# Two attention blocks in one kernel: another order of the second block's two-step cycle, with the last two heads' row maxima taken together in every other step

## The chip, the cores and the metric

The kernel runs on 1 core of one Trainium2 chip. The metric is device time in microseconds (us). The time before is 1884.33 us, the median of 3 runs (1877.62 to 1885.6).

Engines are named as in the profile: PE (TensorE matmul), PEld (its weight loads), DVE (VectorE), ACT (ScalarE), POOL (GpSimd), SP (the engine that issues the DMAs).

## The reference

Two independent multi-head attentions, each with its own input of 2048 tokens by 512 and its own weights, 32 heads of 16. Block A looks back over a window of 256 keys, block B over all 2048 keys. Their outputs are joined along the last axis.

```python
def _B_ref(x, wqkv, wo):
    B, S, D = x.shape            # 1, 2048, 512
    H = 32
    Dh = D // H
    qkv = (lambda x, *d: x.transpose(*d))((x @ wqkv).reshape(B, S, 3, H, Dh), 2, 0, 3, 1, 4)
    q, k, v = qkv[0], qkv[1], qkv[2]
    scores = jnp.einsum("bhqd,bhkd->bhqk", q, k) * (Dh ** -0.5)
    p = _softmax(scores, axis=-1)
    o = jnp.einsum("bhqk,bhkd->bhqd", p, v)
    return (lambda x, *d: x.transpose(*d))(o, 0, 2, 1, 3).reshape(B, S, D) @ wo
```

`_A_ref` is the same with scores outside the window set to -1e9.

## The kernel before

Work is cut into units: a block, a group of 4 heads, and a chunk of 512 queries. Each block has 8 groups x 4 chunks = 32 units. Block A's units and most projections come first, in an order written out by hand; block B's attention follows in the loop at the end of `attention_kernel` (lines 1009 to 1060), which the change touches.

In block B a unit is 16 steps, one for each tile of 128 keys. What belongs to a step:

- **s** (`scores`, line 501): for one head, a matmul of keys by queries into one PSUM bank (128 keys x 512 queries), then an exponential on ACT (line 508) into the tile `p`. Three banks ("e", 0 to 2) serve in turn. Four s make a step.
- **a digit** (`weigh2`, line 532): the weighted sums of values with the exponentials of two steps earlier; 4 stands for all four quarters of the queries, 2 for two of them. Its result gathers in bank 3 ("o") and is copied out by ACT at the unit's end (line 558).
- **M and m** (`max2`, lines 372 and 376): the row maxima of the *next* unit, which the softmax needs ahead of its scores. An item is 128 queries by 512 keys for the four heads of the group: PE makes the products (line 372), DVE reduces them (line 376). M takes heads 0 and 1 together into banks 4 and 5 and reduces them with one instruction. m takes one head, in turn 2 and 3, into one of the banks 6 and 7 (`room()`, which alternates between them). There is an item in every step, 16 in a unit.

When the 16 items of a unit are done, `max_finish` (line 435) takes the maximum over the key chunks (line 444, DVE) and splits it into three parts on POOL. Two steps later `max_rows` (line 463) runs ahead of the step's first s: a transpose on PE (line 468) into one of the banks 6 and 7, again by `room()`, a copy on ACT (line 470) and two DMAs that write the result as extra rows beside the queries.

The heads of a group lie on two sets of rows: even heads at rows 0 to 50, odd heads at rows 64 to 114 (`ROW = 0, 64`). Heads 0 and 2 thus share the first rows, 1 and 3 the second.

The string `ORDER` sets the order in which PE gets this work; it holds two steps (eight s, eight quarters, two items) and is repeated until all items are done. Then `LAST` takes over, without maxima. Each engine works off its own queue in order, and the waits between engines follow from the tiles and banks that are read and written.

```python
ORDER = "ssm4mssMs2msms2sM"
...
            elif x in "Mm" and nm < len(mx):
                u, g, c, qt, kc = mx[nm]
                if x == "M":
                    h = (0, 1)
                    two = view(("p", 0))
                else:
                    h = (2 + half,)
                    half ^= 1
                    two = room()[1][:, None]
                max2(g, c, qt, kc, h, two)
```

`view(("p", 0))` is banks 4 and 5, `view(("p", 1))` banks 6 and 7.

Of the kernel before, what the change touches and what calls it, by code (L numbers as in the profile page):

```python
# [37 lines left out]
PACE = 16 * STEP  # L38


ORDER = "ssm4mssMs2msms2sM"
LAST = "ssss4"
AHEADM = 4
QU = 2.4
# [77 lines left out]
def attention_kernel(ctx: ExitStack, tc: tile.TileContext, xT, wqk, wv, wo, out):  # L122
# [74 lines left out]
    def view(bank):  # L197
        pool, n = bank
        first, width = {"e": (0, 1), "o": (3, 1), "p": (4, 2), "s": (6, 1)}[pool]
        n = first + width * n + (pool == "e" and n > 2)  # L200
        return ps_all[:, n] if width == 1 else ps_all[:, n:n + 2]
# [159 lines left out]
    def max2(g, c, qt, kc, heads, ps):  # L361

        m = maxima(1, g, c).rearrange("p (a r) q k -> p a r q k", a=2)
        early = g == 0 and c == 0 and heads[0] < 2
        if not early:
            follow(("k", 1, g))
            follow(("q", 1, g, c))
        for n, j in enumerate(heads):
            r, a = divmod(j, 2)
            rows = slice(ROW[a], ROW[a] + KS)  # L370
            q, k = (qe[0], ke()) if early else (opq[1, g, c][:, r], opk2(g)[:, r])
            nc.tensor.matmul(ps[:, n], q[rows, 128 * qt:128 * qt + 128], k[rows, kc * QC:kc * QC + QC], start=True,  # L372
                             stop=True)
            t = M.pe("h", 118, 0 if early else loaded(1, g, c))
        r, a = divmod(heads[0], 2)
        nc.vector.tensor_reduce(out=m[:, a:a + len(heads), r, qt, kc], in_=ps, axis=AX.X, op=ALU.max)  # L376
        return M.run("DVE", 65 + 533 * len(heads), t)
# [85 lines left out]
    def max_rows(b, g, c):  # L463
        n = f"{b}_{g}_{c}"
        nm = parts["nm"]
        bank, ps = room()
        ps = ps.bitcast(BF16)
        nc.tensor.transpose(ps[:48, :128], nm.rearrange("p a s j q -> p (a s j q)"), ident)  # L468
        nt = sb.tile([48, 128], F32, name=f"ntr_{n}", tag="ntr")
        nc.scalar.activation(nt, ps[:48, :128], AF.Copy)  # L470
        t = M.run("ACT", 200, M.pe("f", 60, ready["nm", b, g, c]))
        release(bank, t)
        for a in range(2):
            ready["q", b, g, c] = M.dma(12, t)
            nc.sync.dma_start(opq[b, g, c][ROW[a] + KS:ROW[a] + KM].bitcast(F32).rearrange(
                "s r (q t) -> s (r q) t", t=128), nt[24 * a:24 * a + 24])
# [14 lines left out]
    def scores(b, g, c, kt, j, heads=1, pieces=((),)):  # L491

        n = f"{b}_{g}_{c}_{kt}"
        pr, a0 = divmod(j, 2)
        banks = [M.take("e") for _ in range(heads)]
        ps = [view(bank) for bank in banks]
        w = QC if b else sum(x[3] for x in pieces)
        for k, col, q0, n1 in [(kt, 0, 0, QC)] if b else pieces:
            for x in range(heads):
                rows = slice(ROW[a0 + x], ROW[a0 + x] + KM)  # L500
                nc.tensor.matmul(ps[x][:, col:col + n1], opk2(g)[rows, pr, 128 * k:128 * k + 128],  # L501
                                 opq[b, g, c][rows, pr, q0:q0 + n1], start=True, stop=True)
            t = M.pe("h", 235 if b else 12 + n1 / 2.4, ready["q", b, g, c])
        if a0 == 0:
            pts[b, g, c, kt, pr] = sb.tile([128, 2, QC], F32, name=f"p_{n}_{pr}", tag="p", bufs=2 * AHEAD)
        p = pts[b, g, c, kt, pr]
        for x in range(heads):
            nc.scalar.activation(p[:, a0 + x, :w], ps[x][:, :w], AF.Exp, scale=SCALE)  # L508
            done = M.run("ACT", 60 + w / 1.2, t)
            M.release(banks[x], done)  # L510
        if b == 0:

            for d, sign, base in ((0, 1, 0), (2, -1, -1)):
                cols = [col // 128 + x for k, col, q0, n1 in pieces for x in range(n1 // 128)
                        if 4 * c + q0 // 128 + x - k == d]
                for x in cols:
                    v = p[:, :, 128 * x:128 * x + 128]
                    nc.gpsimd.affine_select(out=v, in_=v, pattern=[[0, 2], [sign, 128]], compare_op=ALU.is_ge,  # L518
                                            fill=zero_fill, base=base, channel_multiplier=-sign)
                    done = M.run("Pool", 360, done)  # L520
        ready["p", b, g, c, kt] = done

    def weigh2(g, c, kt, q0, q1):

        follow(("v", 1, g // 2))
        if kt == 0 and q0 == 0:
            obank[0] = M.take("o")
            pvt[1, g, c] = view(obank[0])
        o = pvt[1, g, c]
        for j in range(HG):  # L530
            vc = VW * (HG * (g % 2) + j)
            nc.tensor.matmul(o[32 * j:32 * j + 32, q0:q1], vt[(g // 2) % 2][:, kt, vc:vc + 32],  # L532
                             pts[1, g, c, kt, j // 2][:, j % 2, q0:q1], start=kt == 0 and q0 == 0,
                             stop=kt == NT - 1, skip_group_check=True)
        M.pe("c", 1.7 * (q1 - q0) + 50, ready["p", 1, g, c, kt], ready["v", 1, g // 2, kt])
# [147 lines left out]
    def settle():  # L683

        while soon and soon[0][0] <= M.t["PE"]:
            heapq.heappop(soon)[2]()
# [18 lines left out]
    def room():  # L705

        if slot[0]:
            slot[1] ^= 1
            return None, view(("s", slot[1]))
        while bank() >= M.NEVER:  # L710
            advance()
        b = M.take(pool())
        return b, view(b)[:, 0] if b[0] == "p" else view(b)
# [5 lines left out]
    def pop():  # L719
        now[0], _, f, a = heapq.heappop(todo)  # L720
        f(*a)
        made.add((f, *a))
# [149 lines left out]
    nm = k = nb = ne = 0  # L872
# [18 lines left out]
    while todo_a or gen[0]:  # L891
# [7 lines left out]
        x = "p" if gen[0] else todo_a[0]  # L899
# [105 lines left out]
    mx = [(NA + 1 + i // 16, *units[NA + 1 + i // 16][1:], *divmod(i % 16, NQC)) for i in range(16 * turn)]  # L1005
    ns, nq, nm, half, got = 0, -8, AHEADM, 0, 0
    t0 = M.t["PE"]
    rows = []
    while nq < 4 * len(steps):
        if nm == len(mx) and len(M.banks["e"]) == 3:  # L1010
            M.banks["e"] += [M.t["PE"]] * 2
        for x in ORDER if nm < len(mx) else LAST:
            k = ns // HG
            if x == "s" and k < len(steps):
                if ns % HG == 0:
                    t = k * STEP
                    M.t["PE"] = max(M.t["PE"], t0 + int(1000 * k * STEP))
                    settle()
                    while todo and todo[0][0] <= t:
                        pop()  # L1020
                    if rows and rows[0][0] <= k:
                        max_rows(*rows.pop(0)[1])
                scores(1, *steps[k], ns % HG)
                ns += 1
            elif x in "Mm" and nm < len(mx):
                u, g, c, qt, kc = mx[nm]
                if x == "M":
                    h = (0, 1)
                    two = view(("p", 0))
                else:  # L1030
                    h = (2 + half,)
                    half ^= 1
                    two = room()[1][:, None]
                max2(g, c, qt, kc, h, two)
                got += len(h)
                if got == HG:
                    nm += 1
                    got = 0
                    if nm % 16 == 0:
                        max_finish(1, g, c)  # L1040
                        rows.append((k + 2, (1, g, c)))
            elif x.isdigit():
                if 0 <= nq < 4 * len(steps):
                    g, c, kt = steps[nq // 4]
                    q = nq % 4
                    weigh2(g, c, kt, 128 * q, 128 * (q + int(x)))
                    if kt == NT - 1 and q + int(x) == 4:
                        unit_end(1, g, c)
                nq += int(x)
                if int(x) == 4:  # L1050

                    t = k * STEP
                    two = heapq.nsmallest(2, proj)
                    if two and two[-1][0] <= t and max(operands(y[3]) for y in two) <= M.t["PE"]:
                        now[0] = t
                        for _ in two:
                            advance()
                            while gen[0]:
                                advance()
                            t0 += 2400  # L1060
# [29 lines left out]
```

## Time and profile before

| | |
|---|---|
| median of 3 runs | 1884.33 us (1877.62 to 1885.6) |
| the profiled execution | 1874.48 us |
| its span, first to last instruction | 1872.8 us |
| granted TensorE clock, mean | 0.995 |
| PE / DVE / ACT / POOL busy, share of the span | 98% / 83% / 75% / 25% |
| last maxima of block B's loop | at about 1782 us of the span |

The profile is of one execution. A row of the groups reads: line, engine, operation, tile written <- tiles read, shapes, count | busy time in all, mean ns of one | idle time of the engine ahead of them and what ended it. The chain of waits is the work that ended last, followed back: each piece with its start, its length and what it was. In a timeline the rows are in order of start, and equal instructions that overlap or follow each other stand in one row with their count, the start of the first and the time to the end of the last.

### The profile page before, as it was taken

What the parts mean: (1) busy time and instruction counts of PE and PEld (TensorE: products, weight loads), DVE (VectorE), ACT (ScalarE), POOL (GpSimd) and SP (SyncE); (2) the same over time, 40 slices, a digit from 0 to 9 for tenths busy, and PEclk for the clock granted to TensorE, in tenths of its full rate; (3) what the DMA queues carried; (4) which work ended last, traced back from release to release, by engine and by line L of the source; (5) the groups of instructions that cost most, each with busy time, mean ns of one, the idle gap of its engine ahead of it and who ended that gap; (6) DMA issues with size and microseconds to landing.
All of it is one profiled execution on the core that took longest, in us unless ns stands there. A gap on an engine that the chain in (4) does not pass through costs nothing.

```text
span 1872.8 us, 37299 instructions
## 1 busy us (share of the span) xinstructions
PE 1838.9 (98%) x14376; PEld 926.7 (49%) x14376; DVE 1547.6 (83%) x2320; ACT 1408.5 (75%) x2754; POOL 468.7 (25%) x896
## 2 busy tenths in 40 slices
PE   8999989999999999999999999999999999999999
PEld 6666555666664554544444444444444444444446
DVE  4666677766779777799999999999999999999911
ACT  4356655655548777788888888888888888888883
POOL 0267777655572332000000000100000000000010
PEclk9999999999999999999999999999999999999999
DMA  8665656545554222411310132121031121010102
GB/s 258 182 193 174 204 174 203 171 124 158 171 176 109 92 89 68 95 28 34 61 36 16 36 59 48 28 62 29 16 73 28 34 62 36 16 39 21 31 30 96
DMA packets 129137, 166.68 MB, mean 89 GB/s; under 512 B 22996, under 2 KB 58836, under 8 KB 128948
## 3 DMA queue, kind: packets, MB, share of 16 engines
q1 hardware_dynamic: 128960, 164.31, 30.7%
q8 instruction: 113, 1.85, 0.4%
q14 instruction: 64, 0.52, 0.1%
HBM read 94.49 MB, written 68.19 MB: 87 GB/s over the span
## 4 chain that ended last, share of the span: by engine, by line
PE 91%; DVE 5%; DMA 1%; ACT 1%; issue 1%; SPq 1%; POOL 0%; ACTq 0%; POOLq 0%
PE ps_all L532 29%; PE ps_all L372 19%; PE ps_all L186 18%; PE ps_all L501 18%; PE ps_all L547 4%; PE ps_all L420 3%; DVE mt L376 2%; DVE mt L430 1%; DVE ps_all L429 1%; ACT p L508 1%; PE ps_all L468 1%; DMA vt<-vd 1%; DVE nm L460 0%; DMA in<-xT_A 0%; DVE nr L458 0%
## 5 line engine op out<-in xcount | busy, mean ns | idle before, releaser
L508 ACT ACTIVATE p<-ps_all 128x512 f32<-128x512 f32 x2432 | 1261.5, 600 | 179.7 <-PE ps_all L501 121.0
L376 DVE TENSOR_REDUCE mt<-ps_all 128x2 f32<-128x1024 f32 x1516 | 1202.0, 866 | 79.0 <-PE ps_all L501 52.1
L501 PE MATMUL ps_all<-oq,opk 51*128 51x512 f32 (+2 forms) x2752 | 780.1, 410 | 8.6 <-ACT p L508 5.8
L372 PE MATMUL ps_all<-opk,oq 48*128 48x512 f32 x2016 | 678.1, 439 | 2.0 <-DVE mt L376 1.9
L532 PE MATMUL ps_all<-p,vt 128*32 128x256 f32 (+1 forms) x6056 | 598.3, 467 | 0.5 <-ACT ou L558 0.5
L501 PEld LDWEIGHTS ps_all<-oq,opk 51*128 51x128 f32 x2752 | 396.8, 185 | 205.4 <-ACT p L508 181.9
L372 PEld LDWEIGHTS ps_all<-opk,oq 48*128 48x128 f32 x2016 | 313.2, 185 | 319.9 <-issue 144.2
L453 POOL TENSOR_SCALAR mm<-mm 128x16 f32<-128x16 f32 x31 | 7.8, 253 | 977.5 <-PE ps_all L501 769.3
L518 POOL TENSOR_SCALAR_AFFINE_SELECT p<-p 128x256 f32<-128x256 f32 x480 | 179.6, 407 | 210.5 <-ACT p L508 148.5
L532 PEld LDWEIGHTS ps_all<-p,vt 128*32 128x32 f32 x6056 | 119.6, 108 | 219.1 <-issue 208.5
L186 PE MATMUL ps_all<-x,w 128*128 128x512 f32 x768 | 197.6, 407 | 9.0 <-ACT w L140 9.0
L429 DVE COPY_PREDICATED ps_all<-mone,ps_all 128x256 f32<-128x256 uint16 x224 | 94.8, 423 | 103.1 <-PE ps_all L420 102.5
L186 PEld LDWEIGHTS ps_all<-x,w 128*128 128x128 f32 x768 | 142.9, 192 | 49.4 <-ACT w L140 9.0
L430 DVE TENSOR_REDUCE mt<-ps_all 128x2 f32<-128x512 f32 x224 | 155.2, 693 | 7.7
L248 ACT ACTIVATE raw<-ps_all 128x512 f32<-128x512 f32 x56 | 33.5, 598 | 111.0 <-PE ps_all L186 109.3
L420 PE MATMUL ps_all<-opk,oq 48*128 48x384 f32 (+2 forms) x512 | 91.8, 377 | 9.1 <-DVE mt L430 7.8
L547 PE MATMUL ps_all<-p,vt 128*32 128x384 f32 (+2 forms) x1408 | 98.6, 393 | 0.3 <-POOL p L518 0.3
L186 PE MATMUL ps_all<-w_v,x 128*128 128x512 f32 x384 | 95.1, 398 | 0.2 <-ACT p L508 0.2
L186 PE MATMUL ps_all<-w_o,x_o 128*128 128x512 f32 x384 | 90.4, 393 | 0.0
L186 PEld LDWEIGHTS ps_all<-w_o,x_o 128*128 128x128 f32 x384 | 71.2, 188 | 23.7 <-issue 8.4
L186 PEld LDWEIGHTS ps_all<-w_v,x 128*128 128x128 f32 x384 | 70.2, 188 | 18.7 <-issue 1.9
L259 POOL TENSOR_TENSOR st<-raw,st 128x512 fp32r<-128x512 f32 x56 | 72.0, 1285 | 4.7
(58 smaller groups left out, 588.6 us busy)
## 6 DMA issues: line engine op xcount, KB each, us to landing
parts<-st SPq DMA_DIRECT2D x64, 512.0 KB
oq<-parts SPq DMA_DIRECT2D x128, 128.0 KB
opk<-parts SPq DMA_DIRECT2D x128, 128.0 KB
od<-ou SPq DMA_DIRECT2D x64, 256.0 KB
vd<-vst SPq DMA_DIRECT2D x32, 272.0 KB
oq<-parts SPq DMA_DIRECT2D x128, 64.0 KB
opk<-parts SPq DMA_DIRECT2D x128, 64.0 KB
t<-od SPq DMA_DIRECT2D x32, 256.0 KB
```

The source lines that it names most:

```text
L186: nc.tensor.matmul(ps, l(u), r(v), start=start and k == 0, stop=stop and k == n - 1)
L259: nc.gpsimd.tensor_sub(two[:, 1], raw, two[:, 0].bitcast(F32))
L372: nc.tensor.matmul(ps[:, n], q[rows, 128 * qt:128 * qt + 128], k[rows, kc * QC:kc * QC + QC], start=True, stop=True)
L376: nc.vector.tensor_reduce(out=m[:, a:a + len(heads), r, qt, kc], in_=ps, axis=AX.X, op=ALU.max)
L420: nc.tensor.matmul(two[:, a, 0:w], opq[b, g, c][rows, r, 128 * qt:128 * qt + 128], opk2(g)[rows, r, t0:t1], start=True, stop=True)
L429: nc.vector.copy_predicated(two[:, :, 256:384], later, two[:, :, 0:128])
L430: nc.vector.tensor_reduce(out=m[:, :, r, qt, 0], in_=two[:, :, 128:384], axis=AX.X, op=ALU.max)
L501: nc.tensor.matmul(ps[x][:, col:col + n1], opk2(g)[rows, pr, 128 * k:128 * k + 128], opq[b, g, c][rows, pr, q0:q0 + n1], start=True, stop= ...
L508: nc.scalar.activation(p[:, a0 + x, :w], ps[x][:, :w], AF.Exp, scale=SCALE)
L518: nc.gpsimd.affine_select(out=v, in_=v, pattern=[[0, 2], [sign, 128]], compare_op=ALU.is_ge, fill=zero_fill, base=base, channel_multiplier ...
L532: nc.tensor.matmul(o[32 * j:32 * j + 32, q0:q1], vt[(g // 2) % 2][:, kt, vc:vc + 32], pts[1, g, c, kt, j // 2][:, j % 2, q0:q1], start=kt ...
L547: nc.tensor.matmul(o[32 * j:32 * j + 32, q0:q0 + w], vt[(g // 2) % 2][:, kt, vc:vc + 32], pts[b, g, c, m, j // 2][:, j % 2, col:col + w], ...
```

## The change

The order string is another, and a new letter N takes heads 2 and 3 of an item together, into banks 6 and 7, as M does heads 0 and 1 in banks 4 and 5. In the first step of a cycle the item is M m m as before; in the second it is M N. The counts of scores, weighings and items in a cycle are the same; DVE gets five reductions in place of six.

```diff
-ORDER = "ssm4mssMs2msms2sM"
+ORDER = "sMss4msssmM2ssN2"
@@
-            elif x in "Mm" and nm < len(mx):
+            elif x in "MNm" and nm < len(mx):
                 u, g, c, qt, kc = mx[nm]
                 if x == "M":
                     h = (0, 1)
                     two = view(("p", 0))
+                elif x == "N":
+                    h = (2, 3)
+                    two = view(("p", 1))
                 else:
                     h = (2 + half,)
                     half ^= 1
```

On PE, the middle of a cycle in block B's unit of group 4, chunk 1 before the change. In `p_4_1_12_0` the numbers are group, chunk, key tile and pair of heads; line 532 weighs, line 501 makes scores, line 372 the products for the maxima:

```order
L532 MATMUL ps_all<-p_4_1_12_0_14041,vt_75 32x512 x2
L532 MATMUL ps_all<-p_4_1_12_1_14055,vt_75 32x512 x2
L372 MATMUL ps_all<-opk_73,oq_4_3_13635 128x512
L501 MATMUL ps_all<-oq_4_1_12813,opk_73 128x512 x2
L372 MATMUL ps_all<-opk_73,oq_4_3_13635 128x512 x2
L501 MATMUL ps_all<-oq_4_1_12813,opk_73 128x512
L532 MATMUL ps_all<-p_4_1_13_0_14063,vt_75 32x256 x2
L532 MATMUL ps_all<-p_4_1_13_1_14076,vt_75 32x256 x2
```

The same place of PE's order after the change:

```order
L532 MATMUL ps_all<-p_4_1_12_0_13899,vt_75 32x512 x2
L532 MATMUL ps_all<-p_4_1_12_1_13908,vt_75 32x512 x2
L372 MATMUL ps_all<-opk_73,oq_4_3_13505 128x512
L501 MATMUL ps_all<-oq_4_1_12695,opk_73 128x512 x3
L372 MATMUL ps_all<-opk_73,oq_4_3_13505 128x512 x3
L532 MATMUL ps_all<-p_4_1_13_0_13919,vt_75 32x256 x2
L532 MATMUL ps_all<-p_4_1_13_1_13933,vt_75 32x256 x2
```

Between the two weighings stood six matmuls (m s s M M s, with M as two); now there are seven (m s s s m M M).

The second place is the transpose on PE (line 468) at a cycle's start, before the change:

```order
L532 MATMUL ps_all<-p_4_1_11_1_14015,vt_75 32x256 x2
L501 MATMUL ps_all<-oq_4_1_12813,opk_73 128x512
L372 MATMUL ps_all<-opk_73,oq_4_3_13635 128x512 x2
L468 LDWEIGHTS nm_4_2_14028
L468 MATMUL ps_all<-ident,nm_4_2_14028 48x128
L501 MATMUL ps_all<-oq_4_1_12813,opk_73 128x512 x2
L372 MATMUL ps_all<-opk_73,oq_4_3_13635 128x512
L532 MATMUL ps_all<-p_4_1_12_0_14041,vt_75 32x512 x2
```

And the same transpose after it, where the `x2` of line 372 ahead of the weighing is N:

```order
L501 MATMUL ps_all<-oq_4_1_12695,opk_73 128x512 x2
L372 MATMUL ps_all<-opk_73,oq_4_3_13505 128x512 x2
L532 MATMUL ps_all<-p_4_1_11_0_13859,vt_75 32x256 x2
L532 MATMUL ps_all<-p_4_1_11_1_13873,vt_75 32x256 x2
L468 LDWEIGHTS nm_4_2_13882
L468 MATMUL ps_all<-ident,nm_4_2_13882 48x128
L501 MATMUL ps_all<-oq_4_1_12695,opk_73 128x512
L372 MATMUL ps_all<-opk_73,oq_4_3_13505 128x512 x2
L501 MATMUL ps_all<-oq_4_1_12695,opk_73 128x512 x2
L532 MATMUL ps_all<-p_4_1_12_0_13899,vt_75 32x512 x2
```

The transpose moved from the middle of a group of scores and maxima to the head of one, right behind a weighing; the last maxima ahead of it were a single and an M, and are now an N.

## The prediction

> **What bounds the kernel now.** I read the page's busy shares first, then a table of windows to find the stage that the change touches, then that stage by instruction, then the chain of waits through it, slot by slot.
>
> ```profile
> PE 1838.9 (98%) x14376; PEld 926.7 (49%) x14376; DVE 1547.6 (83%) x2320; ACT 1408.5 (75%) x2754; POOL 468.7 (25%) x896
> L376 DVE TENSOR_REDUCE mt<-ps_all 128x2 f32<-128x1024 f32 x1516 | 1202.0, 866 | 79.0 <-PE ps_all L501 52.1
> ```
>
> The page names PE, but its busy ends are modelled, so 98% is not proof. The second row counts the changed operation: 1516 row-maximum reductions. 40 of them are made ahead of the loop (32 for the first unit of block B, 8 for the next unit's first four items), which leaves 1476; at six in a cycle that is **246 cycles of the order string**. The windows (columns: length, then busy time of PE, PEld, DVE, ACT, POOL, then clock, DMA share, GB/s) and the groups of the second one, 16 units or 128 cycles long, by shape:
>
> ```profile
> 604.00:1072.50 468.50, 468.48 (x3767) 210.48 (x3766) 420.68 (x551) 384.94 (x752) 65.68 (x106) 1.00 0.20 54
> 1072.50:1682.07 609.57, 609.55 (x5139) 252.81 (x5137) 603.39 (x793) 540.86 (x1057) 42.36 (x104) 1.00 0.17 42
> ...
> L508 ACT ACTIVATE p<-ps_all 128x512 f32<-128x512 f32 x1025 | 533.3, 600 | 68.7 <-PE ps_all L501 39.4 <-PE ps_all L372 13.2
> ...
> L376 DVE TENSOR_REDUCE mt<-ps_all 128x1 f32<-128x512 f32 x512 | 327.6, 677 | 4.5 <-PE ps_all L501 3.4 <-PE ps_all L372 1.1
> L376 DVE TENSOR_REDUCE mt<-ps_all 128x2 f32<-128x1024 f32 x257 | 311.9, 1214 | 0.0
> ...
> L558 ACT ACTIVATE ou<-ps_all 128x512 f32<-128x512 f32 x16 | 9.7, 609 | 0.0
> ...
> L470 ACT ACTIVATE ntr<-ps_all 48x128 f32<-48x128 bf16 x16 | 4.1, 257 | 0.0
> ...
> L444 DVE TENSOR_REDUCE mm<-mt 128x16 f32<-128x64 f32 x16 | 3.5, 219 | 1.7
> ...
> L584 DVE RECIPROCAL rd<-ld 128x32 f32<-128x32 f32 x8 | 2.7, 339 | 0.0
> ```
>
> A cycle lasts 609.57/128 = 4.76 us, a unit of eight cycles 38.10. DVE is busy 603.39 of 609.57 us, so DVE is full as well. How long it really holds for one reduction comes from its timeline, where two that overlap stand in one row:
>
> ```profile
> 1004.47 1.27 DVE L376 TENSOR_REDUCE mt<-ps_all 128x1 f32<-128x512 f32 x2
> ...
> 1005.67 1.81 DVE L376 TENSOR_REDUCE mt<-ps_all 128x2 f32<-128x1024 f32 x2
> ```
>
> Two singles end 1.27 us after the first started; less the 0.68 of the second, they start **0.60** apart. A pair with a single behind it takes 1.81, less 0.68 is **1.13**. DVE's floor for a cycle of two pairs and four singles is 2x1.13 + 4x0.60 = 4.66.
>
> PE's floor comes from the chain of waits over one cycle (start, length, what):
>
> ```profile
> 1005.78 0.99 PE ps_all L532 x8
> 1006.78 0.42 PE ps_all L372
> 1007.20 0.24 PE ps_all L501 x2
> 1007.44 0.24 PE ps_all L372 x2
> 1007.68 0.57 PE ps_all L532 x8
> 1008.25 0.67 PE ps_all L372 x2
> 1008.92 0.57 PE ps_all L532 x8
> 1009.49 0.67 PE ps_all L501 x2
> 1010.16 0.23 PE ps_all L372 x2
> 1010.39 1.00 PE ps_all L532 x8
> ```
>
> This is 4.61 us from 1005.78 to 1010.39, with no wait in it. Sixteen score and maximum matmuls (lines 501 and 372) stand there in three groups between the weighings (line 532), and the groups take 0.90, 0.67 and 0.90. They hold 6, 4 and 6 matmuls: the first two of a group take 0.42-0.43 together, every further two 0.23-0.24. Two matmuls in the time of one are possible because even heads lie on rows 0 and up, odd heads on rows 64 and up. I call the time of such a pair a **slot**: now 3 + 2 + 3 = 8. So PE (4.61) and DVE (4.66) are within 0.05 us of each other, and an edit that helps one and hurts the other has to be counted on both.
>
> **The change, part by part.**
>
> *DVE.* In every second step two singles become a pair: 2x0.60 - 1.13 = 0.07 us saved, a cycle falls from 4.66 to 3x1.13 + 2x0.60 = 4.59. If DVE alone set the pace, that would be 246x0.07 = 17 us. [...]
>
> *PE's slots.* Matmuls issue in order. Write 0 and 1 for even and odd heads. Before, a cycle is 1 0 1 0 1 0 | 0 1 1 0 | 1 0 1 0 1 0: whoever pairs off neighbours finds 3, 2 and 3 mixed pairs. After, with the groups from the rows of the two orders:
> - s M s s: 0, 0 1, 1 0. The second 0 must wait for the first, so the first runs alone: 3 slots for five matmuls, 0.90 us.
> - m s s s m M: 0 1, 0 1, 1 0, 1. Four slots for seven, the last one alone: 0.42 + 3x0.24 = 1.13.
> - s s N: 0 1, 0 1: two slots, 0.67.
>
> That is 9 slots. The weighings stay 0.99 + 0.57 + 0.57. **PE's cycle: 4.61 + 0.235 = 4.845**, now clearly above DVE's 4.59. That a lone matmul costs a whole slot shows where a transpose cuts a group:
>
> ```profile
> 1023.49 0.42 PE ps_all L501
> 1023.91 0.23 PE ps_all L372 x2
> 1024.14 0.22 PE ps_all L468
> 1024.36 0.43 PE ps_all L501 x2
> 1024.79 0.45 PE ps_all L372
> 1025.24 1.00 PE ps_all L532 x8
> ```
>
> Here the order is s3 M0 M1, transpose, s0 s1 m. M1 has no partner and takes 0.23 on the chain. The group takes 1.75 instead of 0.90: this cut costs 0.85 in each unit today.
>
> *The transpose (line 468).* It takes a bank of the two in which the single maxima stand (banks 6 and 7). Today it waits a little for a single; the same place on both engines' timelines:
>
> ```profile
> 1023.55 0.59 PE L372 MATMUL ps_all<-opk,oq 48*128 48x512 f32 x2
> 1024.14 0.22 PE L468 MATMUL ps_all<-ident,nm 128*48 128x128 bf16 x1
> 1024.29 0.50 PE L501 MATMUL ps_all<-oq,opk 51*128 51x512 f32 x2
> ...
> 1022.28 1.81 DVE L376 TENSOR_REDUCE mt<-ps_all 128x2 f32<-128x1024 f32 x2
> ```
>
> The single behind that pair ends at 1022.28 + 1.81 = 1024.09, the transpose starts at 1024.14, and the next scores 0.15 later. After the change the two banks belong to N, the last reduction of the cycle, and only a weighing of 0.57 lies between N and the transpose. When does N end? Count from the start of the group s M s s. DVE has slack in the new cycle and waits for the first m, whose matmul starts after 0.90 + 0.99 = 1.89 and is readable about 0.53 later (0.50 a first matmul, 0.03-0.05 a semaphore, as between 1024.09 and 1024.14): 2.42. Then come m 0.60, m 0.60, M 1.13, so N starts at 4.75, ends 1.21 later at 5.96, and frees the transpose at 6.01. Its own turn would be at 4.845: it waits 1.17. Behind it in PE's queue stand all of the next cycle's matmuls, so the wait is on the path. With the 0.15 of the transpose itself: **1.32 a unit**, for 0.85 now. The bounds: 0.15 if N is done in time, 0.15 + N's whole 1.21 behind a late start (some 1.7) if DVE lags. I take 1.32, which both timelines give.
>
> *What costs nothing.* ACT's exponentials come in bursts of three now, where PE has three banks for scores. 533.3/1025 = 0.52 us each, eight make 4.2 of 4.85, and the third's bank is free about 0.1 us before the sixth score wants it. That cover is thin: once a unit the 0.61 us copy of line 558 stands in ACT's queue and may add up to 0.4 us there, up to 12 us in all. DVE's reciprocals (0.34 us) fall into its new slack of 0.25 a cycle. The row-maximum chain through POOL keeps a whole cycle. DMA share is 0.17, and every transfer keeps its step.
>
> *Sum.* A unit after: 8x4.845 + 1.32 = 40.08; before 38.10; +1.98. For 246/8 = 30.75 units: **+61 us**. I carry it over the earlier window too, where PE is full (468.48 of 468.50) and the interleaved projections do not change. The profiled execution took 1874.48 us (span 1872.8), so 1935.5; the median shown is 1884.33, 10 us higher, which gives 1945. I forecast 1940.
>
> **Rivals** (their times by the profiled execution)**.**
> 1. *DVE is the bound and PE finds its pairs anyway* (faster). If PE could bring forward a matmul of the free row group, 8 slots would remain; if the transpose then also found its bank free, a unit would be DVE's 8x4.59 + 0.22 + 0.17 = 37.1, or -31 us: 1844. It decides once PE's cycle stays under 4.66. For it: DVE's 99%. Against it: in the cut group M1 ran alone although an s0 of the other rows stood just behind the transpose, and every group of the chain fits in-order pairs. [...] Chance 0.06.
> 2. *Pairs hold, but the transpose waits*: 8x4.61 + 1.32 = 38.2, +3 us: 1878, no change. Chance 0.04.
> 3. *Nine slots, no wait at the transpose* because DVE runs ahead: 8x4.845 + 0.15 = 38.91, +25 us: 1900. Against it: DVE cannot start m before PE has made it. Chance 0.14.
> 4. *Nine slots and a further wait in every cycle*, as when the third score bank comes 0.1 us late: 246x0.1 = 25 us on top, 1960 (1970 by the median). Chance 0.14.
>
> **How the numbers follow.** The forecast keeps 0.62. Rivals 3 and 4 are sizes of the same sign, so the range takes them in: 1899 to 1963; it leaves out rivals 1 and 2 and the far side of 4. About 0.5% (9 us) is what a measurement here can tell from no change. Slower by more than that: 0.62 + 0.14 + 0.14 = 0.90; within it 0.04; faster 0.06.
>
> **What would show it.** In the new chain of waits: a cycle of 4.82 to 4.87 with groups of 0.90, 1.13 and 0.67; a lone line 501 at the head of one group and a lone line 372 at the end of another; the transpose waiting for DVE's line 376 by over 1 us once a unit, where the cycle lasts some 6.2; DVE's share down to about 93% of the window. The forecast is wrong if the regular cycle stays under 4.7, or if the transpose starts within 0.4 us of the weighing ahead of it.

## The result, and the profile after

The changed kernel takes 1968.62 us (median of 4 runs, 1963.11 to 1973.81), the kernel before 1880.97 us (4 runs): a ratio of **1.0457**, 95% interval 1.0425 to 1.0488. It is slower, as forecast, by 88 us; the forecast was 61 us on the profiled execution, and 1968.62 lies 6 us above the top of the range. The profiled execution took 1971.54 us, 97 more than that of before. (Executions more than 1.5% above the fastest of the same kernel are left out of the ratios; that is so for two of the four in experiment 6, and nowhere else.)

The page's busy line, the long window of block B's loop, and its groups by shape:

```profile
PE 1904.2 (97%) x14376; PEld 966.4 (49%) x14376; DVE 1552.4 (79%) x2074; ACT 1431.4 (73%) x2754; POOL 468.5 (24%) x896
...
1072.50:1682.07 609.57, 592.37 (x4777) 254.02 (x4777) 564.99 (x619) 513.96 (x983) 41.18 (x99) 0.99 0.17 39
...
L508 ACT ACTIVATE p<-ps_all 128x512 f32<-128x512 f32 x953 | 505.1, 599 | 79.3 <-PE ps_all L501 37.7 <-PE ps_all L372 22.4
...
L376 DVE TENSOR_REDUCE mt<-ps_all 128x2 f32<-128x1024 f32 x358 | 417.8, 1217 | 13.7 <-PE ps_all L501 12.7 <-PE ps_all L372 1.0
L376 DVE TENSOR_REDUCE mt<-ps_all 128x1 f32<-128x512 f32 x238 | 155.3, 685 | 28.9 <-PE ps_all L501 19.6 <-PE ps_all L372 8.0
...
L468 PE MATMUL ps_all<-ident,nm 128*48 128x128 bf16 x15 | 3.2, 216 | 17.2 <-DVE mt L376 17.2
```

953 exponentials where there were 1025: at 64 a unit, a unit takes 609.57/14.89 = 40.9 us, not 38.1. DVE is busy 93% of the window, not 99%, and now waits for PE. The transpose (line 468) leaves PE idle for 17.2/15 = 1.15 us each time; in the same window of the kernel before PE had no idle time ahead of it:

```profile
L468 PE MATMUL ps_all<-ident,nm 128*48 128x128 bf16 x16 | 3.5, 216 | 0.0
```

The chain of waits over one regular cycle of the changed kernel:

```profile
1088.06 1.00 PE ps_all L532 x8
1089.06 0.43 PE ps_all L372
1089.49 0.26 PE ps_all L501 x3
1089.75 0.46 PE ps_all L372 x3
1090.21 0.57 PE ps_all L532 x8
1090.78 0.43 PE ps_all L501
1091.20 0.24 PE ps_all L372 x2
1091.44 0.57 PE ps_all L532 x8
1092.01 0.43 PE ps_all L501
1092.44 0.24 PE ps_all L372 x2
1092.68 0.24 PE ps_all L501 x2
1092.92 1.00 PE ps_all L532 x8
```

It is 4.86 us long, and the three groups of scores and maxima between the weighings (line 532) take 1.15, 0.67 and 0.91 us: four slots, two and three. The same chain where the transpose comes:

```profile
1098.78 0.48 PE ps_all L372
1099.26 3.56 DVE mt L376 x4
1102.90 0.22 DVE mm L444
1103.12 4.60 DVE mt L376 x5
1107.77 0.22 PE ps_all L468
1107.98 0.43 PE ps_all L501
...
1108.88 1.84 PE ps_all L532 x8
1110.72 0.72 PE ps_all L372
```

From a single's matmul at 1098.78 on, the chain runs through DVE for two cycles, until N is done and the transpose may start: nine maximum reductions, with the 0.22 us of line 444 among them. Behind it stands what I had not counted: the weighing of four quarters takes 1.84 us instead of 1.00. The timeline shows N on DVE and the transpose on PE. The two windows show the clock (the number behind the five busy times) at the loop's start and right after this wait:

```profile
1106.49 1.22 DVE L376 TENSOR_REDUCE mt<-ps_all 128x2 f32<-128x1024 f32 x1
1107.77 0.22 PE L468 MATMUL ps_all<-ident,nm 128*48 128x128 bf16 x1 [1.15 <-DVE mt L376]
...
566.00:600.00 34.00, 34.00 (x151) 12.96 (x149) 21.33 (x24) 18.05 (x35) 3.16 (x3) 0.50 0.39 84
...
1109.00:1112.40 3.40, 3.40 (x15) 1.16 (x7) 1.61 (x2) 1.90 (x5) 0.00 (x0) 0.51 0.03 7
```

N ends at 1106.49 + 1.22 = 1107.71, the transpose starts at 1107.77. From 1109 to 1112.4 PE has half its clock. It also had half its clock through the loop's first 34 us.

For the experiments, here are the eight cycles of one unit in four of the kernels, in us, measured from the start of one four-quarter weighing to the next in the trace (the sixth cycle holds the transpose):

```
before                  4.61 4.60 4.61 4.64 4.71 5.50 4.66 4.67
changed                 5.07 4.86 4.87 4.86 4.87 6.23 4.85 4.88
changed, 2 units before 5.06 4.86 4.87 4.87 4.85 6.24 4.88 4.89
  the unit in between                            6.23 6.41 4.89
e1_bank4                5.06 4.86 4.97 4.86 4.88 5.28 4.85 4.89
e3_order_alone          5.07 4.86 4.96 4.87 4.86 5.75 4.87 4.90
```

### The profile page after: what moved, and what is told of

Its sections match the earlier page's. It is cut to its first block, busy times and chain, and to the rows that moved or that the text cites. A ratio compares the mean times of both kernels' runs of the same rounds, so it can differ in the third digit from the quotient of the medians.

```text
span 1969.8 us, 37042 instructions
## 1 busy us (share of the span) xinstructions
PE 1904.2 (97%) x14376; PEld 966.4 (49%) x14376; DVE 1552.4 (79%) x2074; ACT 1431.4 (73%) x2754; POOL 468.5 (24%) x896
## 4 chain that ended last, share of the span: by engine, by line
PE 82%; DVE 16%; ACT 1%; issue 1%; DMA 0%; SPq 0%; DVEq 0%; ACTq 0%
PE ps_all L532 24%; PE ps_all L501 18%; PE ps_all L186 18%; PE ps_all L372 15%; DVE mt L376 12%; PE ps_all L547 4%; PE ps_all L420 3%; DVE mt L430 1%; DVE ps_all L429 1%; PE ps_all L468 1%; ACT p L508 1%; DMA in<-xT_A 0%; DVE nm L460 0%; DVE nm L457 0%; DVE mm L444 0%
## 5 line engine op out<-in xcount | busy, mean ns | idle before, releaser
L508 ACT ACTIVATE p<-ps_all 128x512 f32<-128x512 f32 x2432 | 1280.7, 599 | 219.5 <-PE ps_all L501 120.1
L501 PE MATMUL ps_all<-oq,opk 51*128 51x512 f32 (+2 forms) x2752 | 679.6, 422 | 6.4 <-ACT p L508 6.0
L532 PE MATMUL ps_all<-p,vt 128*32 128x256 f32 (+1 forms) x6056 | 608.7, 474 | 0.5 <-ACT ou L558 0.5
L372 PE MATMUL ps_all<-opk,oq 48*128 48x512 f32 x2016 | 576.3, 430 | 1.8 <-DVE mt L376 1.2
L501 PEld LDWEIGHTS ps_all<-oq,opk 51*128 51x128 f32 x2752 | 358.1, 187 | 314.4 <-ACT p L508 278.0
L372 PEld LDWEIGHTS ps_all<-opk,oq 48*128 48x128 f32 x2016 | 267.4, 189 | 233.5 <-DVE mt L376 163.2
```

## The experiments

**1. The transpose's wait taken away.** The transpose goes to bank 4, which M's reduction has left by then.

```diff
-        bank, ps = room()
+        bank, ps = (None, ps_all[:, 4]) if slot[0] else room()
```

> The changed kernel, with one edit: in block B's loop the transpose of line 468 takes bank 4 (which M uses) instead of the bank of N. Theory (nine slots on PE plus the transpose's wait for N plus a slower clock after that wait): the transpose starts within 0.4 us of its turn, a unit loses about 1.0 us of its 1.3, and the 3.4 us stretches at half clock that follow some of the long waits go away too. 30 x 1.0 + about 9 = 39 us less than the changed kernel: 1930 us; regular cycles stay at 4.86. Rival (nine slots are all, the transpose's wait only takes the place of other waits): 1960 us or more. Rival (the maxima of the next cycle now wait for the transpose's copy on ACT): the wait moves to line 372 and the time stays at 1965.

1928.11 us (1925.76 to 1932.46), 1.0262 of before (1.0226 to 1.0299). The transpose's row and the window from 900 to 1700 us:

```profile
L468 PE MATMUL ps_all<-ident,nm 128*48 128x128 bf16 x16 | 3.5, 216 | 0.2
...
900.00:1700.00 800.00, 799.71 (x6489) 342.57 (x6489) 765.20 (x840) 699.03 (x1334) 52.93 (x130) 1.00 0.16 38
```

The wait is gone (0.2 us in 16), the transpose's cycle falls from 6.23 to 5.28, the clock stays at 1.00, and the regular cycles stay at 4.86. So the wait, with what the clock does behind it, is worth some 40 of the 88 us; 48 belong to something else.

**2. The order alone, with and without that wait.** N is taken apart into two singles, the order stays. In the second kernel the transpose also goes to bank 4, as above.

```diff
-ORDER = "sMss4msssmM2ssN2"
+ORDER = "sMss4msssmM2ssmm2"
```

> The order of the change, with N taken apart into two singles again (sMss4msssmM2ssmm2): the merge undone, the order kept. Theory of slots: regular cycles stay at 4.84 to 4.88, as nine slots are nine slots; the transpose waits only for the first of the two singles, some 0.5 us less than for N; 1925 to 1945 us, more than half of the loss. Rival (the merge with its long hold of two banks is the cause): cycles of 4.65 to 4.70 and 1885 us.

> The order of the change with N taken apart into two singles, and the transpose in bank 4: the order alone, without the transpose's wait. If the merge into N neither gains nor costs anything by itself (DVE is not the bound, 4.66 or 4.59 us of work in a cycle of 4.86), this is the same as the changed kernel with the transpose in bank 4: 1928 us, regular cycles 4.86, and the whole of that loss of 48 us belongs to the order's ninth slot and ACT's bursts. Rival (DVE's load still matters behind PE): 6 to 15 us slower than that, 1934 to 1943.

1946.31 us, 1.035 (1.0312 to 1.0388), and 1932.54 us, 1.0278 (1.0253 to 1.0304). The waits of the first from 900 to 1700 us:

```profile
PE ps_all L468 <- DVE mt L376: 12.3, 20, 0.6
```

The transpose waits 12.3/20 = 0.6 us for a single, where it waited 1.15 for N. The second kernel cannot be told from experiment 1 (1.0262, the intervals overlap): without the transpose's wait, no difference shows between two singles and their merge. The order's own cost, then, is the 48 to 54 us by which these two kernels (experiment 1's and this one) are slower than the one before, and the merge's cost in this order is that its bank keeps the transpose waiting longer.

**3. The merge alone,** in the order of before.

```diff
-ORDER = "ssm4mssMs2msms2sM"
+ORDER = "ssm4mssMs2sNs2sM"
```

> The order of before, with one edit: in the second step the two singles become N, where the first of them stood (ssm4mssMs2sNs2sM). PE keeps its eight slots (5 + 1 heads pair off as before), DVE saves 0.07 us a cycle. Theory of banks: N holds banks 6 and 7 until its 1.13 us reduction is done, and it is reduced late, behind M, so the first single of the next cycle has to wait some 0.25 us: cycles of 4.85, units of 39.5, 1920 us. Rival (DVE's load sets the pace, one instruction fewer is a gain): cycles of 4.61, 1865 us.

1946.27 us, 1.0353 (1.0318 to 1.0389): slower, and by more than I had worked out. The end of the group ahead of the four-quarter weighing:

```profile
1075.02 0.23 PE ps_all L501 x2
1075.25 0.37 PE ps_all L372
1075.62 0.99 PE ps_all L532 x8
```

The first single after N, which should pair with the second score, comes alone and takes 0.37: it had to wait until N was reduced and its bank was free. Cycles last 4.97, so 0.36 more than 4.61, not the 0.25 of the expectation. The rest is in the timeline: the weights of the score beside it were loaded from 0.11 us ahead of its matmul, which took 0.39, while those of the held single load at 1075.12, as its matmul starts, and that takes 0.50. One reduction fewer on an engine that was 99% busy made the kernel slower.

**4. What a lone matmul costs,** by adding matmuls. An M makes one of its two products twice; its result is the same. First one more in every cycle of the kernel before (17 matmuls), where it leaves the next score without a partner (the edit is shortened to the lines that matter):

```diff
-        for n, j in enumerate(heads):
+        for n in turns or range(len(heads)):
+            j = heads[n]
@@
+                turns = None
+                if x == "M":
+                    turns = ((0, 1, 0), None)[ms % 2]
+                    ms += 1
-                max2(g, c, qt, kc, h, two)
+                max2(g, c, qt, kc, h, two, turns)
```

> The kernel before, with one matmul more in every cycle: the M behind the weighing of four quarters makes head 0's product twice (0, 1, 0), which leaves the s behind it without a partner. 17 matmuls, nine slots, the order of before and six reductions. Theory of slots: PE's cycle goes from 4.61 to 4.84, a unit from 38.1 to 39.6, 1925 us. Rival (a matmul costs its share, and PE has 0.05 us to spare behind DVE): cycles of 4.7, 1895 us. Rival (DVE is the bound): the same as before, 1880 us.

1919.17 us, 1.02 (1.017 to 1.0229). The group behind the weighing (line numbers are one higher in this kernel):

```profile
1073.19 1.00 PE ps_all L533 x8
1074.18 0.43 PE ps_all L373
...
1074.61 0.47 PE ps_all L373 x3
1075.08 0.24 PE ps_all L502
1075.32 0.57 PE ps_all L533 x8
```

Seven matmuls take 1.14, where the six took 0.90: one matmul more, one slot more, and regular cycles of 4.83 to 4.85. Then two more in every cycle of the kernel of experiment 1 (18 matmuls), so that both lone ones get a partner; the edit differs in one line:

```diff
-                    turns = ((0, 1, 0), None)[ms % 2]
+                    turns = ((1, 0, 1), (0, 1, 0))[ms % 2]
```

> The changed kernel with the transpose in bank 4, and two matmuls more in every cycle: each M makes one of its two products twice (the first M heads 1, 0, 1, the second 0, 1, 0), so that both lone matmuls get a partner on the other rows. 18 matmuls in place of 16, the same result. Theory of slots: nine slots are nine slots, regular cycles stay at 4.86 and the time at 1928 to 1933 us. Rival (every matmul costs its share of PE, 0.12 us): cycles of 5.1, +58 us, 1986 us.

1937.55 us, 1.03 (1.0274 to 1.0327):

```profile
1077.74 0.99 PE ps_all L533 x8
1078.74 0.43 PE ps_all L373
1079.17 0.25 PE ps_all L502 x3
1079.42 0.47 PE ps_all L373 x4
1079.89 0.57 PE ps_all L533 x8
```

Eight matmuls take 1.15, as seven did. Two matmuls more cost 0.04 us a cycle (4.90 for 4.86), 9 us in all, where their shares would have cost 58. The half slots of the new order stand empty. What no run here tells apart is whether neighbours must match in order or only the number in a group counts: in every group of these kernels, five matmuls as three slots or seven as four, both rules give the same.

**5. The wait alone, in the order of before.** The edit of experiment 1, made in the kernel before: there bank 4 belongs to an M whose reduction has hardly begun.

> The kernel before, with its own order, and the transpose in bank 4, where it has to wait for M's reduction: the wait alone, with eight slots. The transpose waits 1.5 to 1.7 us longer than before, once a unit: +43 to +52 us. If such a wait is what makes the clock drop, half-clock stretches of 3.4 us appear in this trace too, beside the transposes, and the clock is below that of before: 1925 to 1940 us. Rival (the clock drops belong to the new order): the loss without any drop after the loop's start, 1922 us. Rival (the wait is taken up by DVE's backlog): under 1895.

1992.95 us (1981.02 to 1997.02), 1.0594 (1.0561 to 1.0627), far more than the wait. Its waits and its window from 900 to 1700 us:

```profile
PE ps_all L468 <- DVE mt L376: 31.1, 18, 1.7
...
900.00:1700.00 800.00, 767.16 (x6141) 309.27 (x6139) 725.63 (x949) 650.27 (x1264) 55.92 (x133) 0.94 0.16 37
```

The eight slots are there (most cycles away from the transposes last 4.60 to 4.74, as before), yet the granted clock is 0.94 in the window, 0.951 in the whole. The trace has stretches of 3.4 to 13.7 us at half clock behind nearly every transpose. They belong to the wait, not to the new order. Two whole units without such a stretch take 39.5 and 39.7 us, where the kernel before takes 38.0 to 38.2, so the wait alone costs about 1.5 us a unit, some 45 us; most other units take 41.0 to 44.2.

The length of the wait matters. Waits of 1.7 us brought the clock down 24 times in 27; those of 1.15 us in the changed kernel 4 times in 20 between 900 and 1700 us (6 in 30 over the loop, where the first three waits are of 1.0 to 1.1 us); those of 0.6 us in the first kernel of experiment 2 never. Nor did the drops come at just any place in time. In the trace's clock records every half-clock stretch of the changed kernel's loop starts a multiple of 3.413 us after the first one (566.17 us), and lasts one or ten such periods. The clock fell at six of the seven transposes that had started 0.83 to 1.13 us ahead of such a period's end (the seventh is the loop's first, at 613.07 us, behind a wait of 1.10 us), and at none of the 23 that lay elsewhere in it. In this trace, then, how many drops the kernel took went along with how its units fell on these periods.

**6. The loop's start.** The changed kernel with the order of before in the first eight cycles.

```diff
+FIRST8 = "ssm4mssMs2msms2sM"
@@
-        for x in ORDER if nm < len(mx) else LAST:
+        for x in (FIRST8 if nm < 20 else ORDER) if nm < len(mx) else LAST:
```

> The changed kernel, with the order of before in the loop's first eight cycles. The changed kernel ran its first 34 us of the loop at half clock, the kernel before 7 us. Theory A (the new order, with its lone matmuls, keeps the clock from coming back once it is down): the loop starts at full clock after 7 us as before, 13 to 16 us less than the changed kernel, 1953 us. Theory B (the clock at the loop's start is set by what runs ahead of it, by chance): the same as the changed kernel, 1966 us, with a stretch at half clock of any length.

1.0454 of before (1.0381 to 1.0526), so no gain that can be told. Its executions spread from 1956.54 to 1988.26 us, and its profiled one is the longest, so what follows is told of that one alone. In it the clock came back 14 us after the loop's start and fell again where the order changes, at 613.8 us, behind a wait of 1.3 us for DVE (1.7 us between two matmuls' starts):

```profile
614.00:668.00 54.00, 54.00 (x248) 20.01 (x245) 30.30 (x32) 26.39 (x50) 13.65 (x17) 0.50 0.14 42
```

PE is busy through all of it, at half clock, until a block of projection matmuls begins. This does not decide between theories A and B. For A: the clock came back under the order of before, if after 14 us and not 7, and stayed down for 54 us under the new one. Against A: in experiment 1, with the new order from the start, the first stretch lasts 7 us, and in both kernels of experiment 2 it lasts 17. Nor are the projections what ends it: in the changed kernel the clock came back at 600 us, and the next of them comes at 649. What decides when the clock comes back stays open.

**7. The copy of line 558 on DVE,** in the kernel of experiment 1.

```diff
-        nc.scalar.activation(ou, pvt[b, g, c], AF.Copy)
+        if slot[0]:
+            nc.vector.tensor_copy(ou, pvt[b, g, c])
+        else:
+            nc.scalar.activation(ou, pvt[b, g, c], AF.Copy)
```

> The changed kernel with the transpose in bank 4, and line 558's copy of the unit's result on DVE instead of ACT. Theory (the copy in ACT's queue delays the exponentials, so that the third score bank comes late and PE waits 0.2 us once a unit): the cycle of 5.06 falls to 4.86, 30 x 0.2 = 6 us less, 1922 us. Rival (DVE's 0.6 us make the maxima late): no gain, 1928 us or more.

1946.62 us, 1.0349 (1.0325 to 1.0373), 18 us slower than experiment 1. The cycle of 5.06 did fall to 4.83, as it should if the copy in ACT's queue had cost those 0.2 us. But the next unit's weighing now waits for DVE, and the cycle ahead of it goes from 4.89 to 5.73; the waits from 900 to 1700 us:

```profile
PEld ps_all L532 <- DVE ou L559: 22.9, 20, 1.2
...
PE ps_all L532 <- DVE ou L559: 16.0, 20, 0.8
```

That new wait also gives ACT time to catch up, so this run alone does not prove the copy guilty. The trace of experiment 1 shows it directly: in one such cycle the copy starts at 1175.21 us, six exponentials follow it on ACT without a gap, and a score's weight load at 1177.33 has waited 0.18 us for ACT. PE's new waits of 0.8 us, 20 of them in this window, brought no drop of the clock.

**8. The kernel before, without its cut group.** The transpose goes to bank 4 and stands behind the four-quarter weighing, at the head of a group. (A planned load waits for its buffer's last use in the planner; nothing else changes.)

```diff
-                    if rows and rows[0][0] <= k:
-                        max_rows(*rows.pop(0)[1])
@@
                             t0 += 2400
+                    if rows and rows[0][0] <= k:
+                        max_rows(*rows.pop(0)[1])
```

> The kernel before, with the transpose moved from the middle of a group to the head of the next one, behind the weighing of four quarters, and into bank 4. The group is no longer cut: of the 0.85 us that the transpose costs PE in a unit some 0.4 go away, until DVE's floor (37.7 to 37.9 us a unit, 38.1 now) is met: 6 to 12 us less than before, 1868 to 1874 us. Rival (DVE is the bound and PE's saving is nothing): the same as before. Rival (the row that the transpose makes lands too late for the next unit's scores, as it is made 1.9 us later): slower than before.

1882.27 us against 1878.95, a ratio of 1.003 (1.0013 to 1.0048): nothing gained. That is the first rival of that run, and its trace bears it out: DVE is busy 790.24 of the 800 us from 900 to 1700 us, as before (790.95), while PE's busy time falls from 799.46 to 794.01; the transpose now waits 5.0 us for DVE in 21 units. The other rival, a row that lands too late, shows as a single wait of 0.3 us for that DMA.

No version beat the kernel before.

## Why the prediction missed its range

- **The bound, and the shift from DVE to PE: right.** DVE's share fell to 93%, as forecast, and the merge's 0.07 us a cycle bought nothing (experiments 1 and 2).
- **Nine slots: right.** 4.845 was forecast for the cycle, 4.86 measured, and the groups are 0.91, 1.15 and 0.67 for 0.90, 1.13 and 0.67. That a lone matmul costs a slot was argued from one cut group; experiment 4 shows it from both sides. In the traces of before and after, PE starts the score and maximum matmuls in the order of the string, in all 1426 groups between two weighings and to within 0.012 us (from 604 us to 1780 and 1870). The first two of a group start 0.003 us apart at the median where they lie on different rows, and 0.048 in the 118 groups s M s s from 1072.5 to 1682 us, where both lie on the first rows. That the neighbours pair off in order is still only argued.
- **The transpose's wait: right as idle time, wrong as a price.** 1.17 us of wait were forecast, 1.15 measured, and the cycle is 6.23 (some 6.2 was forecast). The path was a little longer than the one counted: DVE did not wait for the first m of that cycle, as line 444's 0.22 us had filled its slack, so the chain starts a cycle earlier. The step that failed is "1.32 a unit" as the whole cost: PE's waits were counted as time lost, not as something that brings the clock down. A dropped clock makes the next cycle 6.41 instead of 4.86, about 1.5 us. In 4 of 20 units that is 0.3 us a unit, some 9 us in the loop; that alone is more than the 6 us by which the range was missed. Experiment 1 took both away and gained 40 us; 30 times the difference of the cycles, 6.23 - 5.28, is 28.5 of them.
- **"What costs nothing": wrong.** The ACT burst behind line 558's copy was named with up to 0.4 us a unit and left out of the sum. It costs 0.2 (5.06 for 4.86; see experiment 7), 6 us in all.
- **The loop's start: not in the prediction at all.** 34 us at half clock in the profiled execution, where the kernel before had 7 (560 to 580 us, clock 0.83 there); at half the speed the 27 us more cost some 13 us. Whether the change brings this or the one execution had bad luck is open: the four executions' granted clocks run from 0.983, in the profiled one, to 0.989.
- **The sum.** 61 forecast, + 9 + 6 + 13 = 89; the profiled executions differ by 97. Of the other 8, some 4 are the 0.015 us by which each of 246 regular cycles is longer than forecast, and 1 to 2 that the transpose's cycle is 6.23 for 6.17. Some 2 more stand in eight cycles of the earlier window that also hold projection matmuls, over which the forecast was carried unchanged: those without a transpose went from about 10.35 to 10.84 us, 0.25 more than one slot.
- **The rivals.** The fourth had the right sign for what was missing, but the wrong mechanism: no wait in every cycle. The first, eight slots by pairs out of order, is ruled out by the changed kernel's own chain of nine; experiment 4 does not bear on it, as seven matmuls take four slots in any order. The third (no wait at the transpose) is what experiment 1 built, at 1928 us where that rival was priced at 1900: the ACT burst (6 us) and the transpose's remaining 0.42 for 0.15 a unit (8 us) are half of the difference, and some 6 us lie between the profiled execution, by which it was priced, and the median.

## What to carry to other kernels

Where matmuls run in pairs on different rows of the array, count slots, not matmuls: write each group between two weighings down as a string of row sets and pair off neighbours. Here seven matmuls took 1.15 us, as eight did, and six took 0.90: the odd one paid a whole slot for half the work. Before two reductions are merged, ask how long the merged one holds both its buffers and who is next in line for them: here DVE, busy 99% of the window, lost an instruction a cycle, and the kernel went from 1879.75 to 1946.27 us (experiment 3). And ask of a wait on PE whether it costs more than its length: here 20 waits of 0.6 us and 20 of 0.8 us brought no drop of the clock, those of 1.15 us did so 4 times in 20, those of 1.7 us 24 times in 27. Look at the clock behind it, and keep short PE operations that need a buffer away from the buffer that was filled last.

## What the hardware showed that I had not expected

- PE's clock fell to half behind waits that were shorter than the 3.4 us for which it then stayed down at the least: behind 6 of the changed kernel's 30 waits at the transpose (1.0 to 1.16 us), all six on one place of the trace's 3.413 us period, and behind 24 of 27 waits of 1.7 us in experiment 5. Experiments 1 and 5 take the wait away and add it: the clock from 900 to 1700 us was 1.00 and 0.94.
- The half clock lasted although PE was busy without a gap: 34.00 of 34 us in the changed kernel, 54.00 of 54 us in experiment 6. In experiment 1, with the same order, it lasted 7 us. The spread between executions of one kernel (1925 to 1938 us in the second kernel of experiment 2, with a granted clock from 0.995 to 0.989) goes along with the clock. Which condition ends such a stretch was not found.
